# The first load of a weight matrix in one transfer of 128 partitions or in two of 64

## The chip, the cores and the metric

One Trainium2 chip; the kernel runs on one of its cores. The metric is device time in microseconds, lower is better; before the change it is 227.07 us, the median of three runs (227.03 to 227.23).

## The reference

One decode step of a transformer layer for one token, in float32. The attention part and the gated feed-forward part both read the same normalized input and are added to it:

```python
xn = _layernorm(x, axis=-1)
return x + _A_ref(xn, A_k_cache, A_v_cache, A_wq, A_wo) + _B_ref(xn, B_w_gate, B_w_up, B_w_down)

# A: 32 query heads, 4 key/value heads, the last 4096 positions of the cache
q = (x @ wq)                      # wq 1024 x 4096
scores = q k^T * Dh ** -0.5       # softmax over the 4096 positions
o = softmax(scores) v
return o @ wo                     # wo 4096 x 1024
# B: gated feed-forward, 1024 -> 3584 -> 1024
h = _gelu(x @ w_gate) * (x @ w_up)
return h @ w_down
```

With one token every matrix is read once and used for a single row: 94.4 MB come from memory in a run.

## The kernel before

All matrices and the cache windows come through one buffer in on-chip memory, `ring`: 128 partitions of 32768 floats. `PLAN` (lines 269 to 276) lists the loads in their order, each with its place in `ring` and with the load whose use sets its place free. The first two entries, the two halves of wq (512 rows of the matrix each), have nobody to wait for: they are issued at the very start. Everything after them is issued when an earlier load has been used.

`load` (line 313) issues a load on SyncE's DMA queue. A half of wq is seen by `fours` as 128 partitions of 4 matrix rows each, that is 16384 consecutive floats, 64 KiB, per partition, and comes in one transfer of 128 partitions, 8.4 MB. A load of k_cache comes in two transfers, one to the even and one to the odd partitions (lines 322 and 323), a load of v_cache in one, those of w_down in several pieces by columns.

`project` (line 455) uses a load of wq, w_gate or w_up. Of the four matrix rows that a partition holds, TensorE takes two (`blocks`, 8 matmuls of 512 columns for each), and VectorE multiplies the other two with the input and adds them up in `part` (`add_scaled`), which TensorE sums over the partitions afterwards (`projected`). Both read all 128 partitions. They also need `xz`, the normalized input, which `layer_norm` makes from x. The four small loads of x are issued by ScalarE on its own queue.

The order on each engine is the order of the program. `Flow` (line 49) builds the program twice: the first time it notes which operation touches what, and from that it plans each operation's waits on semaphores; the second time it puts them in. Every transfer has a semaphore of its own; an operation that reads what two transfers wrote waits for both. All operations are issued through line 238, so the profile's rows have that line and are told apart by their tiles.

Of the kernel before, what the change touches and what calls it, by code (L numbers as in the profile page):

```python
# [11 lines left out]
P = 128  # L12
# [6 lines left out]
NR = 4  # L19
# [248 lines left out]
RING = 32768  # L268
# [10 lines left out]
def decode_layer(nc, x, k_cache, v_cache, wq, wo, w_gate, w_up, w_down, out):  # L279
# [3 lines left out]
    def fours(w, jj):  # L283
        return w[NR * P * jj:NR * P * (jj + 1), :].rearrange("(p r) n -> p r n", r=NR)


    def windows(cache, i):
        pair = cache[0, 2 * i:2 * i + 2, SK - WIN:, :]
        return pair.rearrange("g (p j) d -> p g (j d)", p=P // 2)


    def grouped(w, start, rows):
        return w[start:start + P * rows, :].rearrange("(p t) n -> p t n", p=P)


    def source(kind, i):
        if kind == "q":
            return fours(wq, i)
        if kind == "g":
            return fours(w_gate, i)  # L300
        if kind[0] == "u":
            return fours(w_up, i)[:, {"u": slice(NR), "ua": slice(2), "ub": slice(2, NR)}[kind]]
        if kind in "kv":
            cache = k_cache if kind == "k" else v_cache
            return windows(cache, i)
        if kind == "o":
            return grouped(wo, P * WIDE * i, WIDE)
        return grouped(w_down, P * sum(DOWN[:i]), DOWN[i])

    ring = stream.tile([P, RING], F32, name="ring")  # L310
    loaded = {}

    def load(key, at):
        kind, i = key
        src = source(*key)
        if kind in "kv":

            loaded[key] = dst = ring[:, at:at + RING // 4]
            if kind == "v":
                nc.sync.dma_start(dst, src)  # L320
            else:
                for odd in range(2):
                    nc.sync.dma_start(dst[odd:P:2], src[:, odd])
            return
        rows, n = src.shape[1:]
        loaded[key] = ring[:, at:at + rows * n]
        dst = loaded[key].rearrange("p (t n) -> p t n", n=n)
        pieces = PIECES[i] if kind == "d" else (0, rows)
        for t, end in zip(pieces, pieces[1:]):
            cuts = 2 if key == ("d", 2) and end == rows else 1  # L330
            for cut in range(cuts):
                cols = slice(cut * n // cuts, (cut + 1) * n // cuts)
                nc.sync.dma_start(dst[:, t:end, cols], src[:, t:end, cols])

    def used(key):

        for new, at, old in PLAN:
            if old == key:
                load(new, at)
# [471 lines left out]
```

## Time and profile before

| | |
|---|---|
| median of three runs | 227.07 us (227.03 to 227.23) |
| the profiled execution's own time | 227.12 us |
| its span, first to last instruction | 225.2 us |
| busy: TensorE matmuls, VectorE, ScalarE | 125.4, 107.7, 28.2 us |
| bytes read from memory | 94.38 MB, 419 GB/s over the span |
| first wq load: issued, first used | 0.73 us, 22.70 us |
| second wq load: first used | 42.01 us |
| last load of w_down: issued, landed | 198.24 us, 222.96 us |

Times in the profile count from the first instruction; the profiled execution's own time is 1.9 us longer than its span. A busy share is an average over stages that have different limits. A transfer appears in three places: as an issue on the queue of the engine that starts it (SPq for SyncE), as packets on the 16 DMA engines (the windows view gives their share and their rate), and as the landing that others wait for. No engine computes for more than 56% of the span.

### The profile page before, as it was taken

Reading aid. Unit: us, or ns where it says so; the run is one execution under the profiler, and the core shown is the slowest. Engines: PE = TensorE matmul, PEld = TensorE weight load, DVE = VectorE, ACT = ScalarE, POOL = GpSimd, SP = SyncE. Lnnn points to the kernel's source line nnn. Section 1 sums busy time; section 2 is a strip of 40 time slices with the busy share of each in tenths; the row PEclk is TensorE's granted clock in tenths of the full one; section 3 lists DMA queues with packets and bytes.
Section 4 is the critical chain, followed back from the end, with each engine's and each line's share of the span. In section 5 each row is a group of like instructions: output and inputs, shape, how many; then the busy total and the mean of one; then the engine's idle time right before and its main releaser. Section 6 shows DMA issues by size and latency. Waiting matters only on the chain.

```text
span 225.2 us, 2481 instructions
## 1 busy us (share of the span) xinstructions
PE 125.4 (56%) x1107; PEld 66.0 (29%) x1107; DVE 107.7 (48%) x133; ACT 28.2 (13%) x54; POOL 0.7 (0%) x6
## 2 busy tenths in 40 slices
PE   0120910538799992999736553236308989700975
PEld 0010200103646651755511110001004887300441
DVE  7030920591215382345139589239608813950931
ACT  2020000002407410464300310000000000000000
POOL 1000000000000000000000000000000000000000
PEclk9999975596959999799988958558955755765699
DMA  9899889799997999998999999999999999998993
GB/s 373 373 396 536 372 384 547 343 402 463 438 489 336 432 439 451 402 516 377 461 390 418 433 463 418 479 422 466 399 442 454 407 442 442 410 442 361 425 404 141
DMA packets 2954, 94.52 MB, mean 420 GB/s; under 512 B 367, under 2 KB 383, under 8 KB 769
## 3 DMA queue, kind: packets, MB, share of 16 engines
q1 hardware_dynamic: 2920, 94.38, 97.5%
q8 instruction: 8, 0.13, 0.2%
q10 hardware_dynamic: 24, 0.01, 0.0%
q14 instruction: 2, 0.01, 0.0%
HBM read 94.38 MB, written 0.00 MB: 419 GB/s over the span
## 4 chain that ended last, share of the span: by engine, by line
DMA 68%; DVE 20%; PE 9%; ACT 1%; issue 1%; SPq 0%; DVEq 0%
DMA ring<-in_B_w_gate 26%; DMA ring<-in_A_wq 18%; DMA ring<-in_A_wo 13%; DVE part L238 13%; DMA ring<-in_B_w_down 11%; PE tp L238 6%; DVE out_part L238 3%; PE out L238 3%; DVE rows L238 2%; DVE g_sb L238 1%; ACT kT L238 1%; DVE hz L238 1%; PE acc L238 0%; DVE kT L238 0%; SPq L238 0%
## 5 line engine op out<-in xcount | busy, mean ns | idle before, releaser
L238 PE MATMUL acc<-ring,xz 128*32 128x512 f32 x176 | 31.5, 811 | 39.4 <-DMA ring<-in_A_wq 22.3
L238 DVE SCALAR_TENSOR_TENSOR part<-ring,xz,part 128x3584 f32<-128x3584 f32 (+1 forms) x9 | 37.2, 4129 | 23.2 <-DMA ring<-in_A_wq 12.5
L238 PEld LDWEIGHTS acc<-ring,xz 128*32 128x32 f32 x176 | 7.1, 139 | 59.6 <-issue 25.6
L238 PE MATMUL tp<-ident,ring 128*128 128x128 f32 x128 | 20.9, 308 | 6.2 <-DMA ring<-in_A_k_cache 4.0
L238 PE MATMUL out<-ring,hz 128*32 128x256 f32 (+1 forms) x176 | 12.3, 426 | 14.2 <-DMA ring<-in_B_w_down 14.0
L238 PEld LDWEIGHTS tp<-ident,ring 128*128 128x128 f32 x128 | 15.5, 156 | 15.7 <-DMA ring<-in_A_k_cache 4.9
L238 DVE SCALAR_TENSOR_TENSOR out_part<-ring,oz,out_part 128x1024 f32<-128x1024 f32 x15 | 19.3, 1284 | 0.5
L238 DVE COPY kT<-tp 128x512 f32<-128x512 f32 x12 | 8.2, 690 | 20.0 <-PE tp L238 20.0
L238 PE MATMUL out<-ring,oz 128*32 128x256 f32 x128 | 12.1, 562 | 9.5 <-DMA ring<-in_A_wo 9.5
L238 ACT ACTIVATE kT<-tp 128x512 f32<-128x512 f32 x20 | 11.6, 596 | 25.8 <-PE tp L238 25.5
L238 PE MATMUL tp<-ident,kT 128*128 128x4 f32 (+2 forms) x56 | 13.1, 366 | 1.3 <-DVE hz L238 1.3
L238 PEld LDWEIGHTS tp<-ident,kT 128*128 128x128 f32 (+1 forms) x56 | 12.8, 319 | 1.9 <-DVE hz L238 1.5
L238 PE MATMUL acc<-part,units 128*32 128x512 f32 x44 | 7.2, 741 | 9.2 <-DVE part L238 9.2
L238 PEld LDWEIGHTS out<-ring,hz 128*32 128x32 f32 x176 | 5.7, 123 | 21.0 <-DMA ring<-in_B_w_down 17.0
L238 DVE SCALAR_TENSOR_TENSOR out_part<-ring,hz,out_part 128x1024 f32<-128x1024 f32 x6 | 7.7, 1285 | 8.0 <-DMA ring<-in_B_w_down 7.8
L238 DVE TENSOR_SCALAR part<-ring,xz 128x3584 f32<-128x3584 f32 (+1 forms) x3 | 6.5, 2171 | 10.4 <-DMA ring<-in_A_wq 7.4
L238 PEld LDWEIGHTS out<-ring,oz 128*32 128x32 f32 x128 | 5.4, 160 | 16.1 <-DMA ring<-in_A_wo 10.4
L238 PE MATMUL s<-kT,qz 128*32 128x512 f32 x64 | 9.4, 714 | 0.0
L238 DVE TENSOR_REDUCE m<-s 128x2 f32<-128x1024 f32 x4 | 4.9, 1224 | 7.5 <-PE s L238 7.5
L238 PE MATMUL o<-ring,pT 128*32 128x128 f32 x256 | 7.8, 274 | 1.0 <-ACT pT L238 1.0
L238 PEld LDWEIGHTS o<-ring,pT 128*32 128x32 f32 x256 | 6.7, 110 | 1.9 <-ACT pT L238 1.9
L238 PE MATMUL tp<-ident,x_rows 2*128 2x2 f32 x4 | 0.6, 252 | 10.5 <-DMA x_rows<-in_A_x 10.5
(88 smaller groups left out, 68.9 us busy)
## 6 DMA issues: line engine op xcount, KB each, us to landing
ring<-in_B_w_gate SPq DMA_DIRECT2D x2, 7168.0 KB, 29.5
ring<-in_A_k_cache SPq DMA_DIRECT2D x4, 2048.0 KB, 18.1
ring<-in_A_v_cache SPq DMA_DIRECT2D x2, 4096.0 KB, 25.3
ring<-in_B_w_up SPq DMA_DIRECT2D x2, 3584.0 KB, 22.5
ring<-in_B_w_up SPq DMA_DIRECT2D x1, 7168.0 KB, 26.0
ring<-in_B_w_down SPq DMA_DIRECT2D x2, 2048.0 KB, 21.6
ring<-in_B_w_down SPq DMA_DIRECT2D x1, 1024.0 KB, 23.9
ring<-in_B_w_down SPq DMA_DIRECT2D x1, 512.0 KB, 24.8
```

The source lines that it names most:

```text
L238: return lambda *a, **k: self.flow.issue(self.engine, lambda: call(*a, **k))
```

## The change

The first load of wq, and only that one, comes in two transfers: first the rows of the even partitions, then those of the odd ones. The destination, the bytes and the rows of 16384 floats are the same. The other loads keep their form.

```diff
     def load(key, at):
         kind, i = key
         src = source(*key)
+        if key == ("q", 0):
+            loaded[key] = dst = ring[:, at:at + RING // 2]
+            for odd in range(2):
+                some = slice(odd, P, 2)
+                nc.sync.dma_start(dst[some].rearrange("p (t n) -> p t n", t=NR), src[some])
+            return
         if kind in "kv":
```

The head of SyncE's queue, from the start of the program; a row is an issue with its tiles, partitions x floats, and a count. Before:

```order
0 L238 DMA ring<-in_A_wq 128x16384 x2
1 L238 DMA ring<-in_A_k_cache 64x8192 x2
2 L238 DMA ring<-in_A_v_cache 128x1x8192
3 L238 DMA ring<-in_B_w_gate 128x14336
4 L238 DMA ring<-in_A_k_cache 64x8192 x2
```

and with the change:

```order
0 L238 DMA ring<-in_A_wq 64x16384 x2
1 L238 DMA ring<-in_A_wq 128x16384
2 L238 DMA ring<-in_A_k_cache 64x8192 x2
3 L238 DMA ring<-in_A_v_cache 128x1x8192
4 L238 DMA ring<-in_B_w_gate 128x14336
```

There is one issue more ahead of the second load of wq; the rest of the queue is as it was.

VectorE's operations on the two loads of wq, with the semaphores that each waits for (`flow_d_25` and so on are those of transfers, in the order of the program; `flow_e_DVE` is VectorE's own). Before:

```order
29 L238 TENSOR_SCALAR xz<-xc,st 128x8 [waits flow_e_DVE]
30 L238 TENSOR_SCALAR part<-ring,xz 128x4096 [waits flow_d_25,flow_e_DVE]
31 L238 SCALAR_TENSOR_TENSOR part<-ring,xz,part 128x4096 [waits flow_e_DVE]
32 L238 SCALAR_TENSOR_TENSOR part<-ring,xz,part 128x4096 [waits flow_d_26,flow_e_DVE]
33 L238 SCALAR_TENSOR_TENSOR part<-ring,xz,part 128x4096 [waits flow_e_DVE]
```

and with the change:

```order
29 L238 TENSOR_SCALAR xz<-xc,st 128x8 [waits flow_e_DVE]
30 L238 TENSOR_SCALAR part<-ring,xz 128x4096 [waits flow_d_26,flow_d_25,flow_e_DVE]
31 L238 SCALAR_TENSOR_TENSOR part<-ring,xz,part 128x4096 [waits flow_e_DVE]
32 L238 SCALAR_TENSOR_TENSOR part<-ring,xz,part 128x4096 [waits flow_d_27,flow_e_DVE]
33 L238 SCALAR_TENSOR_TENSOR part<-ring,xz,part 128x4096 [waits flow_e_DVE]
```

The first operation on the load waits for two transfers in place of one. TensorE's first matmul on it changes in the same way; no operation of TensorE, VectorE or ScalarE is added or moved.

## The prediction

> **What bounds the kernel now.** I read the page's queue table first, then the transfers by stretch of the span, then the chain of waits. The queue table gives, for each DMA queue, packets, megabytes and the share of the span in which the 16 DMA engines were busy with them:
>
> ```profile
> q1 hardware_dynamic: 2920, 94.38, 97.5%
> ```
>
> SyncE's queue alone keeps the engines busy for 97.5% of the span. Whether the missing 2.5% lies in the middle or at the ends is told by the windows view (start and end, length, busy time of PE, PEld, DVE, ACT, POOL, granted clock, DMA share, GB/s). It counts a packet whole where it begins, so a share can pass 1:
>
> ```profile
> 2.60:21.00 18.40, 1.78 (x8) 1.55 (x8) 4.78 (x27) 2.53 (x4) 0.00 (x0) 1.00 0.92 399
> 21.00:40.90 19.90, 6.01 (x32) 1.51 (x32) 6.84 (x2) 0.00 (x0) 0.00 (x0) 0.75 0.98 422
> 40.90:80.00 39.10, 31.29 (x256) 16.97 (x260) 17.16 (x19) 11.81 (x23) 0.00 (x0) 0.82 1.00 431
> 80.00:120.00 40.00, 29.73 (x349) 17.35 (x340) 17.79 (x21) 10.87 (x23) 0.00 (x0) 0.91 1.01 432
> 120.00:160.00 40.00, 18.26 (x101) 4.28 (x95) 27.25 (x29) 2.54 (x5) 0.00 (x0) 0.74 1.02 442
> 160.00:200.00 40.00, 25.14 (x187) 18.27 (x184) 23.36 (x25) 0.00 (x0) 0.00 (x0) 0.64 0.99 427
> ```
>
> From 21 us to 200 us the share stays between 0.98 and 1.02: the queue never runs dry, whatever the engines compute. (The 0.92 of the first row is the counting: the packets of its first two microseconds began ahead of it.) That the compute engines are ahead of the queue, not behind it, is seen in the chain of waits (start, length, what), whose first large and last large pieces are transfers:
>
> ```profile
> 0.73 0.41 SPq L238
> 1.15 0.06 issue
> 1.21 40.76 DMA ring<-in_A_wq
> ...
> 197.87 0.33 SPq L238
> 198.20 0.04 issue
> 198.24 24.72 DMA ring<-in_B_w_down
> 222.96 0.04 issue
> 223.00 0.47 PE tp L238 x8
> 223.47 0.02 issue
> 223.50 0.29 DVE y_last L238
> ```
>
> The last transfer is issued at 198.24 and lands 24.72 us later, so it stood behind some 24 us of other data. A delay or a gain of a microsecond in an issue is swallowed by that backlog; a delay or a gain in when the data starts to flow isn't, since the same bytes follow without a break. The end is therefore the start of the flow, plus the bytes at the engines' rate, plus a fixed tail. The change touches the start of the flow and nothing else that counts, so I look there closely.
>
> **The start of the flow, in detail.** Two issues of wq stand at the head of SyncE (start, total length, count), and the windows around the first packets read:
>
> ```profile
> 0.73 0.89 SPq L238 DMA_DIRECT2D ring<-in_A_wq  x2
> ...
> 1.20:1.70 0.50, 0.00 (x0) 0.00 (x0) 0.42 (x3) 0.00 (x0) 0.10 (x1) 1.00 0.01 4
> 1.70:2.10 0.40, 0.00 (x0) 0.00 (x0) 0.34 (x1) 0.00 (x0) 0.00 (x0) 1.00 4.76 1638
> 2.10:2.50 0.40, 0.00 (x0) 0.00 (x0) 0.40 (x1) 0.34 (x1) 0.00 (x0) 1.00 2.60 983
> 2.50:4.65 2.15, 0.00 (x0) 0.00 (x0) 1.87 (x11) 0.94 (x1) 0.00 (x0) 1.00 0.00 0
> 4.65:5.25 0.60, 0.00 (x0) 0.00 (x0) 0.57 (x5) 0.00 (x0) 0.00 (x0) 1.00 4.03 1748
> ```
>
> 1638 GB/s over 0.40 us are 655 kB, ten packets of 65.5 kB (one row of 16384 floats); 983 GB/s over 0.40 us are six. So the 16 engines begin their first packet one after another between 1.7 and 2.5 us. Their 16 second packets begin between 4.65 and 5.25. Share times length is a packet's mean time: 4.03 x 0.60 = 2.42 us for the second ones, but 4.76 x 0.40 + 2.60 x 0.40 = 2.94 us for the first: 0.53 us too long on average. Going back by 2.42 us from 4.65 and 5.25, the data moves at full pace only from 2.23 us (first engine) to 2.83 us (last engine).
>
> For comparison, transfers of two rows of 512 bytes on an idle queue, the stores at the end. The rows are their issue and the stretches before and at their packets:
>
> ```profile
> 223.32 0.33 SPq L238 DMA_DIRECT2D out_y<-y  x1
> 223.81 0.26 SPq L238 DMA_DIRECT2D out_y<-y_last  x1
> ...
> 223.65:224.05 0.40, 0.00 (x0) 0.00 (x0) 0.14 (x1) 0.00 (x0) 0.00 (x0) 1.00 0.00 0
> 224.05:224.15 0.10, 0.00 (x0) 0.00 (x0) 0.00 (x0) 0.00 (x0) 0.00 (x0) 1.00 0.09 21
> 224.15:224.53 0.38, 0.00 (x0) 0.00 (x0) 0.00 (x0) 0.00 (x0) 0.00 (x0) 1.00 0.00 0
> 224.53:224.63 0.10, 0.00 (x0) 0.00 (x0) 0.00 (x0) 0.00 (x0) 0.00 (x0) 1.00 0.09 21
> ```
>
> Packets begin about 0.75 us after the start of either issue (0.4 to 0.5 us after its end). The large first transfer needs 2.23 - 0.73 = 1.50 to 2.83 - 0.73 = 2.10 us by the same count: 0.75 to 1.35 us more. My reading is that this extra is the making of its 128 row descriptors, of both the reading and the writing side, and that a packet can't finish before its own are there. The trace doesn't show descriptors, so this is a reading, not a row.
>
> **The change, part by part.** It removes one transfer of 128 rows and adds two of 64 rows of the same length: the same bytes, the same packets, the same engines, one more issue on SyncE.
>
> (1) Earlier flow. If the extra 0.75 to 1.35 us goes with the number of rows, half of it is left for the first transfer: 0.38 to 0.68 us gained. Everything behind it follows without a gap, and the engine that is last counts: up to -0.68 us. The bounds are 0 (the extra doesn't depend on the rows) and -1.35 (it vanishes).
>
> (2) A longer first issue. Transfers into every other partition are in the trace already, those of k_cache. The tile view gives the issue's min, median and max in ns:
>
> ```profile
> L238 SPq DMA_DIRECT2D ring<-in_A_wq x2: 408/410/413, 0.7 to 1.2; - x2
> L238 SPq DMA_DIRECT2D ring<-in_A_k_cache x2: 538/560/581, 26.5 to 27.1; - x2
> L238 SPq DMA_DIRECT2D ring<-in_B_w_gate x1: 334/334/334, 51.1 to 51.1; - x1
> ```
>
> A first issue in that form takes 0.54 us, one of whole partitions 0.33: +0.20 us, if packets are counted from the issue's end. The two stores, 0.33 and 0.26 us long and both 0.75 us from start to packet, speak for counting from the start, so between 0 and +0.20. I take the middle of the two ways for the last engine, -0.68 and (1.25 / 2 = 0.62 from the issue's end at 1.15, where stores need 0.43) -0.62 + 0.20 = -0.42: **-0.55 us**.
>
> (3) The second half and the second load of wq are issued 0.5 to 0.8 us later than wq's second load is now. Each engine then has four packets of 2.42 us to do, 9.7 us: hidden. Without that cover the 0.6 us of one issue would count in full. Behind them on SyncE stands the first load of k_cache, which waits for TensorE at 26.5 us: untouched.
>
> (4) Pace of the 64-row form. With 32.8 kB rows the k_cache packets read:
>
> ```profile
> 42.30:42.90 0.60, 0.60 (x8) 0.03 (x4) 0.60 (x1) 0.00 (x0) 0.00 (x0) 0.50 2.03 874
> ```
>
> 2.03 x 0.60 = 1.218 us for half of a wq row's bytes, so 2.436 us for a whole one, against 2.42: +0.02 us on each of an engine's 8 packets of this load, 0.15 us at most; part of that is the fixed cost of a packet, which wq's longer rows pay half as often. I take +0.05. Between the two halves each engine has one more completion to write; k_cache's pairs already do so, and the share of 1.00 from 40.90 to 80.00 leaves no room for more than hundredths.
>
> (5) One more wait. VectorE's first multiply and TensorE's first matmul on the load now wait for two landings. The first half lands around 12 us (2.5 + 4 x 2.42, an estimate), the second where the whole lands now (the multiply begins at 22.70, below), so the added wait has long passed. Queued behind it on VectorE is the chain of four `part` operations, on TensorE 32 matmuls, and SyncE's k_cache issue behind both; with the backlog a shift of 0.05 us there costs nothing.
>
> ```profile
> 15.08 0.23 DVE L238 TENSOR_SCALAR xz<-xc,st 128x8 f32<-128x8 f32 x1
> ...
> 22.70 2.35 DVE L238 TENSOR_SCALAR part<-ring,xz 128x4096 f32<-128x4096 f32 x1 [7.39 <-DMA ring<-in_A_wq]
> ```
>
> The layer norm's result xz, which it also needs, is there by 15.31 us, so no new wait shows if the load lands half a microsecond sooner.
>
> Sum: -0.55 + 0.05 + 0 = -0.50 us. The profiled execution took 227.12 us, 0.05 above the median of 227.07, so 226.62 for it and about **226.6** for the median, 0.2% faster. Differences under 0.2% (0.45 us) can't be told from no change by this kernel's measurements, and the forecast stands just at that line.
>
> **The rivals.**
>
> No change that can be measured. The first packets may be slow for another reason than their descriptors, for instance because 16 engines begin on a memory that isn't yet streaming; the first of them to start are slowed although their descriptors came first, which fits this as well. Then (1) is 0, (2) and (4) give 0 to +0.25, and the time is 227.07 to 227.3, say 227.15. [...]
>
> Slower. The halves read every other row, so successive packets of an engine, and the 16 engines among themselves, are twice as far apart in memory as now. k_cache can't rule this out, since there each 64-row transfer reads one contiguous block. Rows that show what slow packets of this size cost are the last of wq's second load:
>
> ```profile
> 38.50:39.20 0.70, 0.00 (x0) 0.00 (x0) 0.00 (x0) 0.00 (x0) 0.00 (x0) 0.50 3.53 1498
> ```
>
> 3.53 x 0.70 = 2.47 us, 0.055 above 2.42. Were all 8 packets of an engine so, 0.44 us; with (2) at +0.20, +0.64, and 227.7. Against it: almost all packets of 65.5 kB take 2.42 us, which looks like the engines' own limit with memory to spare. It decides from a mean packet of about 2.45 us, where its 8 x 0.03 and the 0.20 reach the measurable 0.45. [...]
>
> The change doesn't do what it says: 64 rows would be spread over fewer than 16 DMA engines. The k_cache row speaks against it: 874 GB/s over 0.60 us are 524 kB, 16 packets of 32.8 kB, one on each. I leave it no chance of its own.
>
> **How the numbers follow.** The earlier flow has 0.45 and centres on 226.6, from 226.0 (a gain of 1.1, near the bound of (1)) to 226.9. No change has 0.33, from 226.9 to 227.4. Slower has 0.22, around 227.7. The range for 8 times in 10 leaves out the upper half of the slower case and the most extreme gains: 226.1 to 227.7. The first case, whose mechanism is the likeliest to overshoot my half (its bound is 1.35), gives most of its weight to more than 0.2% faster; with the edge of it falling into "within 0.2%", and a little of the slower case too, I put faster at 0.43, within 0.2% at 0.33, slower at 0.24.
>
> **What would show it.** Right: in the changed kernel's windows the 16 second packets begin before about 4.8 us at the latest, the first wq multiply at about 22.2, and the last w_down landing moves by the same half microsecond. Step (1) is wrong if the first packets still average 2.94 us and the second ones begin up to 5.25. The slower rival is right if wq's later packets (7 to 20 us) average over 2.45 us. Wrong in kind I would be if the flow started sooner but the end didn't move: then one engine, delayed elsewhere, sets the end, and the share between 200 and 221 us would fall.

## The result, and the profile after

The changed kernel takes 227.46 us (median of 21 runs, 227.31 to 227.74), the kernel before 227.13 in the same 21 rounds (227.00 to 227.32). The ratio is 1.0015, with a 95% interval of 1.0009 to 1.0021: slower by 0.33 us, where 0.5 us faster was forecast. The profiled execution took 227.45 us, its span 225.6.

The windows view of the changed kernel around the first packets (start and end, length, busy time of PE, PEld, DVE, ACT, POOL, granted clock, DMA share, GB/s; packets counted where they begin):

```profile
1.20:2.00 0.80, 0.00 (x0) 0.00 (x0) 0.66 (x4) 0.00 (x0) 0.10 (x1) 1.00 0.01 3
2.00:2.70 0.70, 0.00 (x0) 0.00 (x0) 0.59 (x1) 0.51 (x1) 0.00 (x0) 1.00 4.47 1498
2.70:5.15 2.45, 0.00 (x0) 0.00 (x0) 2.27 (x12) 0.78 (x1) 0.00 (x0) 1.00 0.00 0
5.15:5.75 0.60, 0.00 (x0) 0.00 (x0) 0.27 (x3) 0.00 (x0) 0.00 (x0) 1.00 4.04 1751
9.95:10.65 0.70, 0.03 (x1) 0.00 (x0) 0.56 (x3) 0.00 (x0) 0.00 (x0) 1.00 3.46 1499
```

No wq packet begins before 2.00 us; before the change they began from 1.7. All 16 first packets begin between 2.00 and 2.70 and take 4.47 x 0.70 = 3.13 us each, no less than the 2.94 of before. The second ones begin from 5.15 to 5.75, where they began from 4.65 to 5.25. From then on a packet takes 2.42 us as before: 3.46 x 0.70 in the last row.

The issues (tile view: count, then min, median and max in ns, first and last start), and the chain of waits at its head and its end (start, length, what):

```profile
L238 SPq DMA_DIRECT2D ring<-in_A_wq x3: 550/584/617, 0.7 to 2.0; - x3
```

```profile
0.73 0.55 SPq L238
1.28 0.05 issue
1.33 0.58 SPq L238
1.92 0.05 issue
1.97 40.41 DMA ring<-in_A_wq
...
198.74 24.53 DMA ring<-in_B_w_down
```

The first issue takes 0.55 us in place of 0.41. The second load of wq lands at 1.97 + 40.41 = 42.38, where it landed at 1.21 + 40.76 = 41.97; the last load of w_down lands at 223.27, before at 222.96. So the first packets begin 0.3 us later and the second ones 0.5, the second load lands 0.41 us later, and at the end 0.31 us of it is left. Nothing between adds to it. Each of these is one execution against one; the medians differ by 0.33. The engines' first use of the load moves as well (the timeline's row of VectorE's first multiply, which was at 22.70):

```profile
23.16 2.35 DVE L238 TENSOR_SCALAR part<-ring,xz 128x4096 f32<-128x4096 f32 x1 [10.01 <-DMA ring<-in_A_wq]
```

### The profile page after: what moved, and what is told of

Same layout as the page of the kernel before. It is cut to its first block, busy times and chain, and to the rows that moved or that the text cites. A ratio compares the mean times of both kernels' runs of the same rounds, so it can differ in the third digit from the quotient of the medians.

```text
span 225.6 us, 2482 instructions
## 1 busy us (share of the span) xinstructions
PE 126.3 (56%) x1107; PEld 66.2 (29%) x1107; DVE 107.6 (48%) x133; ACT 28.4 (13%) x54; POOL 0.7 (0%) x6
## 4 chain that ended last, share of the span: by engine, by line
DMA 56%; PE 20%; DVE 19%; ACT 3%; issue 1%; SPq 1%; DVEq 0%
DMA ring<-in_A_wq 18%; DMA ring<-in_B_w_gate 14%; DMA ring<-in_A_wo 13%; DMA ring<-in_B_w_down 11%; PE tp L238 10%; DVE part L238 10%; PE acc L238 4%; DVE out_part L238 3%; PE out L238 3%; PE s L238 2%; DVE rows L238 2%; ACT kT L238 1%; DVE kT L238 1%; PE o L238 1%; DVE m L238 1%
## 5 line engine op out<-in xcount | busy, mean ns | idle before, releaser
L238 PE MATMUL acc<-ring,xz 128*32 128x512 f32 x176 | 32.1, 819 | 42.1 <-DMA ring<-in_A_wq 24.8
L238 PE MATMUL tp<-ident,ring 128*128 128x128 f32 x128 | 21.6, 319 | 5.7 <-DMA ring<-in_A_k_cache 3.7
L238 PEld LDWEIGHTS tp<-ident,ring 128*128 128x128 f32 x128 | 16.2, 161 | 15.2 <-DMA ring<-in_A_k_cache 4.6
L238 ACT ACTIVATE rows<-acc 128x1024 f32<-128x1024 f32 x1 | 1.0, 1024 | 41.2 <-PE acc L238 41.2
## 6 DMA issues: line engine op xcount, KB each, us to landing
ring<-in_B_w_down SPq DMA_DIRECT2D x2, 2048.0 KB, 21.4
```

Source lines behind the costliest of these rows:

```text
L238: return lambda *a, **k: self.flow.issue(self.engine, lambda: call(*a, **k))
```

## The experiments

**Is the start itself steady?** The kernel before, profiled once more (no edit).

> The kernel before, profiled a second time. In the changed kernel the first packets begin at 2.08 us and the second ones between 5.18 and 5.74, against 1.78 and 4.67 to 5.23 before. Theory (the start of the flow is later in the changed kernel, and that alone is the loss): this profile shows 1.8 and 4.7 to 5.2 again, within 0.05 us. Rival (the start wanders from run to run by some tenths): it lies elsewhere, by 0.2 us or more.

227.19 us, beside 227.19 for the kernel before in the same rounds. Its windows:

```profile
1.70:2.00 0.30, 0.00 (x0) 0.00 (x0) 0.24 (x1) 0.00 (x0) 0.00 (x0) 1.00 7.99 2621
2.00:3.05 1.05, 0.00 (x0) 0.00 (x0) 0.88 (x2) 0.89 (x1) 0.00 (x0) 1.00 0.70 250
4.60:5.70 1.10, 0.00 (x0) 0.00 (x0) 0.82 (x7) 0.00 (x0) 0.00 (x0) 1.00 2.20 953
```

The first packets begin from 1.7 us again (2621 GB/s over 0.30 us are 12 of the 16), and none of the later start of the changed kernel is to be seen. How the 16 are spread over the following 0.7 us does vary from one execution to the next (12 of 16 before 2.00 us here; the prediction's rows have ten of 16 before 2.10), and so does the time that the first packets take: 7.99 x 0.30 + 0.70 x 1.05 = 3.13 us here, where the same kernel had 2.94. So a difference of 0.2 us between two profiles in this stretch means nothing by itself, and the 3.13 us of the changed kernel are no loss of its own.

**Does the step of the partitions matter?** Two transfers of neighbouring partitions.

```diff
-                some = slice(odd, P, 2)
+                some = slice(odd * P // 2, (odd + 1) * P // 2)
```

> The first wq load in two transfers of 64 neighbouring partitions each. Theory A (a transfer of fewer than 128 partitions takes a slower way to its descriptors, whatever the step): issue 0.55 us, first packets at 2.08, time 227.45. Theory B (the step of two partitions is what costs): issue 0.41 us, first packets at 1.78, time 227.1 or below, since there are half the rows.

248.56 us, 1.0942 times the kernel before (1.0927 to 1.0957): neither theory had forecast that. The windows and the issues:

```profile
1.70:2.00 0.30, 0.00 (x0) 0.00 (x0) 0.24 (x1) 0.00 (x0) 0.00 (x0) 1.00 0.00 0
2.00:3.00 1.00, 0.00 (x0) 0.00 (x0) 0.83 (x2) 0.80 (x1) 0.00 (x0) 1.00 4.90 1049
6.60:7.70 1.10, 0.00 (x0) 0.00 (x0) 0.00 (x0) 0.00 (x0) 0.00 (x0) 1.00 4.66 953
11.80:12.80 1.00, 0.00 (x0) 0.00 (x0) 0.00 (x0) 0.00 (x0) 0.00 (x0) 1.00 5.13 1049
```

```profile
L238 SPq DMA_DIRECT2D ring<-in_A_wq x3: 567/584/620, 0.7 to 2.0; - x3
```

Two things are in it. The start is that of the changed kernel: first issue 0.57 us, packets from 2.0, so a step of two isn't needed for the late start. And a packet takes 5.13 us, 2.1 times its usual time, for as long as the load lasts: eight packets on each engine with 2.7 us too much make 21.7 us, and 21.4 were lost.

**Does the split cost where it isn't first?** The same split on the second load of wq.

```diff
-        if key == ("q", 0):
+        if key == ("q", 1):
```

> The even/odd split on the second wq load in place of the first. Theory (only the start of the flow counts, and here the first transfer is the whole one): first packets at 1.78, time 227.1, within 0.1 of before. Rival (the split costs wherever it stands, by its pace, its completion in the middle or its extra wait): 227.4 to 227.5.

227.12 us, ratio 1.0000 (0.9991 to 1.0009). The tile view of its three wq issues has a median of 538 ns and a maximum of 582: the longer issues are there, only they aren't first (the first is the shortest, 408 ns). That puts aside the pace, the completion in the middle and the additional wait as causes, since all of them are in this kernel too.

**Fewer rows first.** 16 partitions, then 112.

```diff
-            for odd in range(2):
-                some = slice(odd, P, 2)
+            for some in (slice(0, 16), slice(16, P)):
```

> The first wq load as 16 partitions and then 112, so that the first transfer has one row for each DMA engine. If the making of descriptors goes with the number of rows, the engines move at full pace some 0.5 us earlier than in the changed kernel: second packets between 4.3 and 4.9, time 226.8 to 227.1. If the delay is a fixed cost of the short form, as with 64 rows: second packets from 5.2, time 227.4 to 227.5. In between, if the second transfer comes too late to follow the first without a gap.

248.76 us, 1.0947 times (1.0932 to 1.0962). It can't answer what it was for, since neighbouring partitions are slow here too, and more so:

```profile
1.70:2.80 1.10, 0.00 (x0) 0.00 (x0) 0.87 (x2) 0.63 (x1) 0.00 (x0) 1.00 7.75 953
9.60:11.40 1.80, 0.00 (x0) 0.00 (x0) 0.00 (x0) 0.00 (x0) 0.00 (x0) 1.00 3.00 584
```

```profile
L238 SPq DMA_DIRECT2D ring<-in_A_wq x3: 398/400/450, 0.7 to 1.6; - x3
```

The 16 packets into 16 neighbouring partitions take 7.75 x 1.10 = 8.5 us each, the next 16, of the other 112, 3.00 x 1.80 = 5.4. But the issues are the short ones, 0.40 us, and the packets begin from 1.7 us. So the late start doesn't belong to "fewer than 128 rows".

**Two transfers of all partitions.** The split by matrix rows.

```diff
-            for odd in range(2):
-                some = slice(odd, P, 2)
-                nc.sync.dma_start(dst[some].rearrange("p (t n) -> p t n", t=NR), src[some])
+            dst = dst.rearrange("p (t n) -> p t n", t=NR)
+            for t in (0, 2):
+                nc.sync.dma_start(dst[:, t:t + 2], src[:, t:t + 2])
```

> The first wq load in two transfers again, but by matrix rows: each has all 128 partitions and 8192 floats of each (packets of 32.8 kB). Theory (the loss is the late start that the 64-row form has): issue 0.41 us, first packets at 1.78, time 227.1 to 227.2. Rival (any second transfer at the head of the queue costs it): 227.4 or more. It also tells what the slow first packet is: if a fixed time is lost in it, it takes 1.21 + 0.5 to 0.7 = 1.7 to 1.9 us; if the first stretch is slow in proportion, 1.5 us.

227.13 us, ratio 0.9996 (0.9987 to 1.0005), and issues of 407 to 421 ns. Two transfers at the head cost nothing in that form. Its windows answer the second question:

```profile
1.70:2.80 1.10, 0.00 (x0) 0.00 (x0) 0.88 (x2) 0.67 (x1) 0.00 (x0) 1.00 1.61 477
3.45:4.20 0.75, 0.00 (x0) 0.00 (x0) 0.67 (x6) 0.00 (x0) 0.00 (x0) 1.00 1.61 699
```

A first packet of half the size takes 1.61 x 1.10 = 1.77 us, a second one 1.61 x 0.75 = 1.21. The excess is 0.56 us; with whole rows it was 0.53 us in the kernel before and 0.71 when it was profiled again. So it doesn't halve with the packet: it is about a fixed time at these two sizes.

**Does a late start pass to the end?** The kernel before with two small loads ahead of wq on SyncE.

```diff
-        nc.scalar.dma_start(
+        nc.sync.dma_start(
             x_out[ROW[c]:ROW[c] + 2, :].rearrange("c (h n) -> c h n", h=2), x_in[c:c + 2]
```

> The kernel before, with the two small loads of x_out (two rows each) issued on SyncE ahead of wq in place of on ScalarE, so that the first wq issue begins later by two issues, 0.5 to 0.6 us. Theory (the start of the flow passes to the end one to one): first wq packets at about 2.3, time 227.6 to 227.75. Rival (a late start is mostly made good by the backlog or hidden): under 227.35.

228.52 us, ratio 1.0060 (1.0047 to 1.0072): 1.35 us more, not 0.5. The timeline and the windows say why:

```profile
1.16 0.64 SPq L238 DMA_DIRECT2D x_out<-in_A_x  x2
1.85 0.83 SPq L238 DMA_DIRECT2D ring<-in_A_wq  x2
```

```profile
2.75:3.35 0.60, 0.60 (x4) 0.52 (x4) 0.59 (x1) 0.07 (x1) 0.00 (x0) 1.00 5.31 1748
```

The small loads wait for the memset of x_out until 1.16 us, so the first wq issue begins at 1.85, 1.12 us later than before, and its packets from 2.75. The last load of w_down, in the chain of waits:

```profile
198.62 25.53 DMA ring<-in_B_w_down
```

It lands at 224.15, 1.19 us later than before, and the span, 226.4 against 225.2, is longer by as much; the rest of the 1.35 us lies outside the span. What the start loses is not made good anywhere.

**Four transfers of 32.** Every fourth partition.

```diff
-            for odd in range(2):
-                some = slice(odd, P, 2)
+            for odd in range(4):
+                some = slice(odd, P, 4)
```

> The first wq load in four transfers of 32 partitions, every fourth one. The packets are those of before, two for each engine and transfer. If the late start belongs to 64 rows alone (16 rows issued in 0.40 us and began at 1.78): first packets at 1.78, time 227.1 to 227.2. If it belongs to transfers into stepped or few partitions: issue 0.55, first packets at 2.08, and 227.4 to 227.5, or more if the following issues of 0.6 us each can't keep the engines fed (each has 4.8 us of work from one).

227.56 us, ratio 1.0018 (1.0009 to 1.0027).

```profile
L238 SPq DMA_DIRECT2D ring<-in_A_wq x5: 556/592/623, 0.7 to 3.3; - x5
```

```profile
1.70:2.00 0.30, 0.00 (x0) 0.00 (x0) 0.24 (x1) 0.00 (x0) 0.00 (x0) 1.00 0.00 0
2.00:3.05 1.05, 0.00 (x0) 0.00 (x0) 0.88 (x2) 0.85 (x1) 0.00 (x0) 1.00 2.92 999
```

The long issue and the late packets again, with a quarter of the rows in place of a half: the start is the same 2.0 us with 32 rows as with 64.

**Which counts are issued quickly?** 96 and 32, and 48 and 80 neighbouring partitions.

```diff
-            for odd in range(2):
-                some = slice(odd, P, 2)
+            for some in (slice(0, 96), slice(96, P)):
```

```diff
+            for some in (slice(0, 48), slice(48, P)):
```

> The first wq load as 96 neighbouring partitions and then 32. Neighbouring partitions make the pace slow (248 us with 64 and 64), so only the issues and the first packets are read. Issues so far: 0.40 us for 16, 112 and 128 rows, 0.55 to 0.58 for 32 and 64. Theory C (only counts that are a small power of two times 16 take the long way): 96 rows 0.40 us with first packets at 1.78, then 32 rows 0.57. Rival D (what the 16 and 112 rows had was something else, and counts below 128 take the long way in general): 96 rows 0.55 us, first packets at 2.08.

> As the run before, with 48 and then 80 partitions (three and five rows for each engine). Theory C: both issues 0.40 us, first packets at 1.78. Rival D: both 0.55 us or more, first packets at 2.08.

One execution each, 247.67 and 256.59 us. The issues, of the kernel with 96 first and of the one with 48:

```profile
L238 SPq DMA_DIRECT2D ring<-in_A_wq x3: 400/406/422, 0.7 to 1.6; - x3
```

```profile
L238 SPq DMA_DIRECT2D ring<-in_A_wq x3: 398/403/445, 0.7 to 1.6; - x3
```

All are short, that of 32 rows too. Rival D falls, and theory C with it: 32 rows are issued in 0.40 to 0.42 us when they are neighbours and in 0.56 when they are every fourth. A count doesn't decide, and neither does the step: 64 neighbouring rows at the head (e2) take 0.57 us. What does decide, no trace shows. Nor is the same form issued quickly in every place: in the changed kernel the second load of wq has the form that took 0.41 us before the change, stands right behind the two halves, and its issue is the longest of the three, 0.62 us.

**A long first issue with all 128 rows.** The kernel before, whole load, one transfer; the edit turns one setting of the build off ahead of that load's issue and on again behind it, and changes nothing else. What the setting makes an issue do, and whether it tells the forms above apart, no trace shows.

> [...] Rival (the number of rows or transfers at the head is the loss): first packets at 1.78, time 227.1 to 227.2.

227.55 us, ratio 1.0015 (1.0006 to 1.0024): the whole loss of the changed kernel, without its change.

```profile
0.73 0.55 SPq L238
1.28 0.06 issue
1.34 41.01 DMA ring<-in_A_wq
...
198.66 24.74 DMA ring<-in_B_w_down
```

```profile
1.70:2.00 0.30, 0.00 (x0) 0.00 (x0) 0.24 (x1) 0.00 (x0) 0.00 (x0) 1.00 0.00 0
2.00:3.05 1.05, 0.00 (x0) 0.00 (x0) 0.88 (x2) 0.86 (x1) 0.00 (x0) 1.00 2.90 999
4.90:5.80 0.90, 0.00 (x0) 0.00 (x0) 0.52 (x4) 0.00 (x0) 0.00 (x0) 1.00 2.69 1167
```

```profile
L238 SPq DMA_DIRECT2D ring<-in_A_wq x2: 548/564/579, 0.7 to 1.3; - x2
```

The same issue of 0.55 us, the same first packets from 2.0 us, the second load landing at 42.35 (42.38 in the changed kernel), the last load of w_down at 223.40 (223.27 there). The rival falls: with all 128 rows in one transfer, that setting alone is enough for the whole loss, so neither fewer rows nor a second transfer is needed for it. That the halves of the changed kernel are slow to start for the same reason is not shown; the two kernels share the rows above. The second issue, 0.58 us, has the form and the setting that gave 0.41 us in the kernel before and is long behind a long one, as in the changed kernel; with eight packets of 2.42 us on each engine ahead of its own data it costs nothing. The reverse, an even/odd half with a short first issue, was not run.

**Why are neighbouring halves slow?** Their source rows are neighbours too; here they are not.

```diff
-                some = slice(odd, P, 2)
-                nc.sync.dma_start(dst[some].rearrange("p (t n) -> p t n", t=NR), src[some])
+                some = slice(odd * P // 2, (odd + 1) * P // 2)
+                nc.sync.dma_start(dst[some].rearrange("p (t n) -> p t n", t=NR), src[odd:P:2])
```

> Two transfers of 64 neighbouring partitions, as in the run of neighbouring halves (packets of 5.12 us, 248.56 us), but filled with the even and then the odd rows of the source, so that partitions hold other matrix rows than the reference needs: the product with wq is another one, the work the same. If the place in on-chip memory that 64 neighbouring partitions share makes them slow: packets of 5.1 us again, 248 to 249. If their neighbouring source rows in memory do: packets of 2.42 us, 227.4.

248.55 us in one execution, 248.56 with neighbouring source rows.

```profile
2.00:3.00 1.00, 0.00 (x0) 0.00 (x0) 0.83 (x2) 0.80 (x1) 0.00 (x0) 1.00 4.78 1049
6.60:7.70 1.10, 0.00 (x0) 0.00 (x0) 0.00 (x0) 0.00 (x0) 0.00 (x0) 1.00 4.38 896
```

The 16 packets of the first row take 4.78 us each. The second row has 15 (896 GB/s over 1.10 us are 986 kB), so 4.38 x 1.10 x 16/15 = 5.14 us for each. The source rows of these transfers are those of the changed kernel, whose packets take 2.42; the destination makes the difference.

## Why the prediction was wrong

*What bounds the kernel* was right: the queue is full from the start of the flow to the end, and a shift of the start reaches the end, +0.31 us at the last landing here and, with the small loads ahead, +1.19 us there for a first issue that begins 1.12 us later.

*Step (1), the earlier flow*, failed, and with it the sign. It read the 0.75 to 1.35 us that the first transfer needs beyond a small one as the making of 128 rows' descriptors, and took half of it off. The runs show none of that: with a first issue of 0.55 to 0.56 us, 128 rows (e10), 64 (the change) and 32 (e7) all have their first packets from 2.0 us, and these take 3.0 to 3.1 us in all three. The excess of the first packet over the later ones is 0.5 to 0.7 us with rows of 64 KiB and 0.56 us with half rows (e5). It is about a fixed time of the first packets, whatever the number of rows. The prediction had the row that spoke against it in its first rival, packets slowed although they began first, and preferred the reading that gave a number.

*Step (2), the longer issue*, had the right mechanism and was mis-sized. Its sign, its form (the k_cache row) and the issue itself, 0.55 us against 0.54 in that row, were right. But its +0.20 us compares the 0.54 with the 0.33 us of w_gate; wq's own first issue, in the same rows, takes 0.41, so the issue could grow by 0.13 to 0.14 us only. And it took the +0.20 us as the upper bound and half of it as the value, arguing from the two stores that packets count from the issue's start. What it cost is 0.3 us or somewhat more: the first packets begin 0.30 us later (2.08 against 1.78, of which the issue has 0.14), because the time between the issue's end and the first packet grows too, from 0.64 to 0.79 us. The stores couldn't tell that: their issues take 0.33 and 0.26 us, so they say nothing of one of 0.55. The k_cache issues couldn't either, since they stand behind other data (issued from 26.5 us, while the second load of wq lands only at 41.97), where no one sees when their first packet could have begun.

*Steps (3) to (5)* held. The second half and the second load follow without a gap, the pace of the even/odd form is 2.42 us, and the added wait costs nothing; e3 has all three and takes 227.12 us.

*The rivals.* No change, at 227.07 to 227.3, came closest and rightly put (1) at zero, since the first packets are no faster with fewer rows (3.0 to 3.1 us with 128, 64 and 32; whether for the reason it named, no run shows), but with (2) at most 0.20 it stopped short of 227.46. The slower one had the right sign for a wrong cause: the packets are not slowed, as its own test shows at 9.95 us, 3.46 x 0.70 = 2.42 us. The measured time lies within the stated range, but on the other side of the time before than the forecast; the range reached that far for the slower rival, whose mechanism did not happen, so that is luck.

What stays open: why the first issue (0.55 in place of 0.41 us) and the time from its end to the first packet (0.79 in place of 0.64) are each some 0.15 us longer, why an unchanged issue right behind it is long too (0.58 and 0.62 us), and why the first packets take half a microsecond more than later ones. All were measured, none taken apart.

## What to carry to other kernels

Where a kernel is bound by a queue that never runs dry, look at the issue of its very first transfer: here its form was worth 0.3 us, and the same form on the second load nothing (e3). Of the forms tried at the head, only loads of all 128 partitions, in one transfer or in two by matrix rows, had both the early start and the full pace, and the one transfer lost the early start by a setting of the build (e10). A price taken from an issue that stands behind a backlog isn't the price at the head, where the time to the first packet counts and not the issue's length: here the issue grew by 0.14 us, the time to the first packet by 0.30. And a split over partitions kept its pace in these runs only where each part took every second or every fourth of the 128: even/odd costs 0.3 us at the head and nothing behind it, neighbouring halves cost 21 us.

## What the runs showed of the hardware

At the head of the queue, SyncE's first issue took 0.41 us in the kernel before, and its first packet began 1.05 us after the issue began (1.78 us); in e4, e5, e8 and e9 the median issue of wq took 0.40 to 0.41 us. In the changed kernel the first issue took 0.55 us and the first packet began after 1.35 us (2.08); in e2, e7 and e10 the shortest issue took 0.55 to 0.57 us and no packet of wq began before 2.00. The same bytes, 128 rows in one transfer, were issued in 0.41 us in the kernel before and in 0.55 in e10, which differ by one setting of the build. An issue unchanged from the kernel before, 0.41 us there, took 0.58 right behind a long one in e10 and 0.62 in the changed kernel.

Transfers into 64 neighbouring partitions ran at half pace, 5.13 us for a packet of 65.5 kB in place of 2.42 (e2), and the packets into 16 took 8.5 us (e4). Transfers into every second partition ran at full pace, 2.42 us, and so did those into every fourth (e7, 16 packets from 4.60 to 5.70 us, 2.20 x 1.10 = 2.42 us). With the source rows spread instead of the partitions the pace stayed low (e11, 5.14 us).
